# First-layer jobs of twice the tiles in an attention and gated feed-forward kernel: one PSUM unit of gates and one of values

## The chip, the cores and the metric

The kernel runs on one core of a Trainium2 chip. The metric is the device time of one execution in microseconds (us); less is better. The names of the profile: PE is TensorE (matmuls) and PEld its weight loads, DVE is VectorE, ACT is ScalarE, POOL is GpSimd, SP is SyncE.

## The reference

Two computations follow each other. First an attention with a block mask, over 4 batches, 8 heads, 768 positions and 64 columns a head; then a feed-forward network with a sigmoid gate over the 3072 tokens.

```python
scores = np.matmul(q, k.transpose(0, 1, 3, 2)) / np.sqrt(64)
scores = np.where(mask, scores, -1e9)    # blocks of 32: neighbours, first and last, 3 sampled ones a row
attn = softmax(scores)                   # over the keys
x = np.matmul(attn, v)                   # -> (3072, 512), heads side by side
gate = 1.0 / (1.0 + np.exp(-(x @ w_gate)))       # 512 -> 1536
out = (gate * (x @ w_val)) @ w_out               # 1536 -> 512
```

## The kernel before

**Units.** The 3072 tokens are 12 units of 256: unit n is a third of the queries of batch n // 3. For each unit and each pair of heads (0 to 3) there are three tasks of scores, `s4.3.2` being unit 4, pair 3, third 2 of the keys. Each is four matmuls into a PSUM unit, one exp of 1024 columns on ACT (L597) that empties it into a buffer P, and, when the three thirds are there, one product of 3072 columns with the mask on DVE (L624). Then come the product of P and v (`pv`), the division by the sums of rows (`nrm`, L649 and L650) and the transposition of x.

**First layer.** `f2.1` is job 1 of group 2. Units 1 to 4 are groups of their own; 5 and 6, 7 and 8, 9 and 10 are groups 5 to 7; `GROUPS` has the list. Before the change a job is one PSUM unit of two banks: one bank takes the gate's products (x times w_gate), the other the values' (x times w_val), 512 columns each, which is two tiles of 128 hidden columns for one unit, or one for a pair. TensorE has 16 matmuls for each half a job. ACT makes a tanh of 512 columns from the gates (L823; the sigmoid is half of 1 plus the tanh of half the input), and DVE multiplies it with the values into `ht` (L826, "the gate" below), after which the PSUM unit is free.

**Second layer.** Units 1 to 10 go in pairs, with seven products in place of eight (`z1` is units 1 and 2, `z2` units 3 and 4, `z4` units 7 and 8; in it A, B, P5, P4 and P3 are products, c11 to c22 what goes out). The sums of blocks that they need are made on DVE (L962, tiles `sums` and `wsum`). Unit 0 (`y0`) and unit 11 (`y_last`) go alone.

**Row tiles.** Most matmuls contract over 64 rows, and two of them stand side by side in the two row halves of the array (`64*128` in the profile). They are recorded by `turns`, in halves a and b, since the two row halves change PSUM banks between them; other work is put in between. The first layers of units 0 and 1 (`WIDE = 2`) use all 128 rows (`128*128`), recorded by `whole`.

**PSUM** is four units of two banks, `m0` to `m3` (m_125 to m_128 where instructions are listed). Whoever takes one waits until its last reader is done.

**The order** is written by hand. All pieces are tasks in a list of class `Plan`; the string `ORDER` says in which order they are recorded. In a token such as `41:3` or `234@249` the number is the task, a letter behind it the engine on which it is done, `:3` the PSUM unit that it takes, and `@249` holds a load until task 249's scores. Each engine runs its own instructions in that order:

```python
            if slot is not None:
                more["take"].slot = int(slot)
            self.last[i] = fn(eng or engines[0][0])
            if gate is not None:
                self.hold(self.last[i], self.last[int(gate)])
```

**Loads and copies.** q, k and v and the weights come by DMA from POOL's queue (L220, L230, L235). POOL, ACT or DVE copy k and q (to `pr`, L277 and L279) and v (to `vex`); k is then transposed by a DMA (`kT<-pr`). For the last unit half of w_out, which the sums of the pairs have overwritten, is loaded again (L1086).

Of the kernel before, what the change touches and what calls it, by code (L numbers as in the profile page):

```python
# [23 lines left out]
NP = H // 2  # L24
# [12 lines left out]
SPLIT, AFTER = 3, (0, 1, 3, 2)  # L37
BIG = 1024.0
# [4 lines left out]
j3 j3 j3 j3 j3 j3 j3 j3 6 17 14 11A 7:0 18:3 8 15:2 19A 16 9:1 23:0 38:3 39 40:2 24 10 21:0 41 86:1  # L43
26:3 87A 82:2 22 27 42:0 46:1 43 47 83 12:3 31:2 13 32 33:0 34 36:3 37 84:2 28:0 62:1 63 85 50:2 51
29 70:0 96@70 20 88:3 44:1 30 71 89 52:2 72:3 90:0 45 73 56:1 91 53 74:3 4@56 0@56 3@56 25 149@56 75
60:2 66:0 80:3 81 57 61 54:1 92:2 48:3 67 111:0 93 112 55 113:1 114 225@113 49 64:3 35 97:2 76:0 65
125@113 98 106:3 77 107 68:1 78:2 69 121:0 79 99:1 122 58:3 100 59 144:2 145 165:1 123:3 124 115
130:0 131 126:2 132 133 147:3 146 166 148 103:0 127 138:1 128 104 134:3 2@103 139 129 109:1 110
1@103 94:0 163:2 135 95 136 179:1 180 164 137 153:0 105 182:1 5@182 154 251:2 252 150:3 183 193:2
151 194 155 167 240:0 241 156:1 152 157 117:2 201 108@240 184:3 191 185 118 187:0 192 158 249:2 202  # L50
169:1 223:3 188 250 140:0 170 224 141 205:2 189:0 171 198@205 206 161G 190 243:3 244 199:0 200 195
172 159:2 258 160A 221:0 173 162 203:3 101:2 186@203 102 245@203 142G 143 238G 222 174 204 218:0 177
196:2 175D 197 259 253 276:3 219 277 207 212:1 282:2 213 214 260A 242 247G 283 209:3 210 211 215:1
261 265:2 216 235 217 266 239 168@265 236 237 273:3 255:1 263:2 274 264 256 119:0 268 120 284:3 269
270 248 285 116@284 328:0 275 329 279 246 229:2 230 231 286 363:1 220G 361:3 362 364 232:0 208@361
325:2 233 326 305:3 226:1 181 234 254@305 300:0 287@305 303:2 306 365 278@303 257G 330@303 227 228
262G 301 304 320 446@303 389:3 449G 390 321 327 322 292:1 380:2 381 293 294 295 331 367:3 410:2 358
178 368 375 432:0 411 280G 370:1 433 376 377 371 296:2 372:0 373 297 267@372 332 366@372 298 333 386
299 383:3 384 288:1 391:0 392 289 316:2 290 302G 435:3 317 382 312:0 437@435 291 412:1 385@412 436
318 681@412 307@412 393 319 323G 313 176 413 314 315 407:3 441:1 442 408 460:2 427 308:0 461 434  # L60
443:1 428 309 444 463:2 399:1 429 438 450:3 310 311 464 335 336 447:0 530:2 281 451 400 445 448
338:3 531 401 402 337 414@530 457:2 324 339 374@457 454 458 341 532:1 533 342 347:2 271G 359A 369
455 272 343 589@532 387G 456 452:1 340 482:0 334 344 348 346 349 453 353:1 459 483 345 539:0 504:3
350 540 430G 505 354 465:0 466 351 484:3 355 378G 395:1 501:0 485 352 480:2 388 467 396 537:3
597@537 481 502 561@537 498 360 397 538 462 398 564G 419:0 503 547:1 548 499 500 558:3 559 420 421
472:1 379 575:2 439 576 422 565:3 473 535:0 566 403:2 536 529 567:3 440 474 534 431 475 404 550:1
542 568 490:3 405 406 394@550 409G 617@550 551 543 544 593:2 491 549 594 492 493 556:1 415:0 553
578:2 557 560 416 579 417 418 423:1 586:3 587 562:2 424 563 425 584:3 585 476:0 426 570 614:1 615
603:3 577 604 571 572 477 468:1 588 581 606:2 478 479 590:3 607 469 591 470 471 598 595:2 596
552@595 599 600 658:0 486:1 605 612:2 696G 554G 633:3 487 632G 659 660@633 613 634 494:0 630:2 495  # L70
488 496 616 489 655:3 497 631 650 506 357 656 592 609 618:1 651 652 676:0 677 507 619 620 356 638:3
580@676 678:0 541@678 639 733:2 679 621 509:1 608@733 640 641 734 747:0 748 742:3 508 510 512D 518:2
582G 583 743 513 511 635:0 727:3 636 569@727 519 514 728 735:0 736 697:3 698 515 516 657 517 626:0
520 740:3 627 730:1 741 628 521 680 694:3 731 629 545G 546 601G 522 695 699:1 674A 700 673 523 755:0
724 555 524:2 725 756 737 767:1 602 768 525 726 622:0 526 753:3 573 574 754 729 661:1 623 624 610
625 646:2 662 663 738:3 750:0 751 647 739 664 648 770:1 744 669:0 649 760:2 771 637@760 527 761 745
762:1 763 670 749 746 671 672 642:2 682:1 643 644 773:3 774 758:0 683 757 759 645 764 848:3 684
665:2 765 752 685 849 686:1 675 666 667 766 769 775:0 668 687 690:3 776 611 688 790:0 653G 654 831:2
691 791 832 777 808 689 811:2 692 693 701 702 772 732 812 778:1 829:3 830 809 850:2 779 851 780 810
782:3 893:2 894 781 704:0 814:1 792:2 793 528 705 703 707D 708 783 815 784 794:2 800:1 795 709 878:2  # L80
# [5 lines left out]
962:0 963 856 864:2 854 926:1 858D 859 921:0 927 922 865 860 920 943:1 945:0 903 944 857 946 861 863  # L86
# [4 lines left out]
1029 1038 1049 1005 1006:0 1031:2 1007 1032 1033 1050 1030 1015:3 1009D 1010 1039:1 1011 1040 1041  # L91
1012 1034 1016 1042 1014 1021:2 1043:1 1008 1017 1022 1018 1023 1025 1044 1026 1019 1045 1013D 1020
1051:2 1052 1046 1053 1054 1056:0 1057 1058 1061:3 1062 1063 1024 1059 1055 1064 1065 1060
# [58 lines left out]
def kernel(  # L152
# [214 lines left out]
    def whole(mms, bank, begins=True, ends=True):  # L367
# [21 lines left out]
    rings["xT"] = [xTs[:, (n + 1) % 6] for n in range(6)]  # L389
    used = {nm: {} for nm in rings}  # L390
# [388 lines left out]
    class Ffn:  # L779
# [16 lines left out]
        def f(self, j):  # L796

            bank = Bank()
            i = len(used["th"])
            th = home("th", i)  # L800
# [77 lines left out]
            c = plan.add(f"f{self.g}.{j}.th", [(ACT, 0.57)], tanh, [a] + before("th", i), free=bank, part=1)  # L878
            g = plan.add(f"f{self.g}.{j}.ga", [(DVE, 0.68)], gate, [c], free=bank, part=1)
            used["th"][i] = [g]  # L880
            for f in tiles:
                self.gated[f] = g
# [65 lines left out]
        def z(self, mate):  # L948
# [132 lines left out]
            if self.z_ == last_z:  # L1081
                back.append(
                    plan.add(
                        "ldw0",
                        [(DMA, 0.72)],
                        lambda eng: nc.gpsimd.dma_start(  # L1086
                            wo[:, 0:HF, UQ : 2 * UQ],
                            moe_w_out.rearrange("(f p) m -> p f m", p=128)[:, 0:HF, UQ : 2 * UQ],
                        ),
                        [pb, t3],  # L1090
                        dma=("L", 0.393),
                    )
                )
# [22 lines left out]
        def y_last(self, i):  # L1116

            n = self.ns[i]
            for s, c0, c1, eng, queue in (
# [6 lines left out]
                for f0 in range(0, NF, 4):  # L1126

                    def go(eng, bank=bank, f0=f0, s=s, c0=c0, c1=c1):
                        for f in range(f0, f0 + 4):
                            tiled(  # L1130
                                both(bank)[:, 0, 0 : c1 - c0],
                                self.ht[:, f, i * UQ + s * 128 : i * UQ + (s + 1) * 128],
                                wo[:, f, c0:c1],
                                f == 0,
                                f == NF - 1,
                            )

                    a = plan.add(
                        f"y{n}.{s}.{c0}.{f0}",
                        [(PE, 4 * Y_WIDE * (c1 - c0) / DM)],  # L1140
                        go,
                        [self.gated[f] for f in range(f0, f0 + 4)] + (back if a is None else [a]),
                        take=bank if f0 == 0 else None,
                        lag=0.0 if f0 < 8 else None,
                        ops=8,
                        wide=True,
                    )
# [188 lines left out]
```

## Time and profile before

| | |
|---|---|
| runs | 282.92, 284.26 and 290.8 us; median 284.26 |
| the profiled execution | 282.64 us, of which 280.9 us is the span of the core |
| clock granted to TensorE in the span | 0.994 |
| instructions | 11919, of them 5459 matmuls, 282 on DVE, 231 on ACT |

The profile is one execution. In its rows a matmul's end is modelled; the starts are measured. "Idle before" is the time in which an engine stood still ahead of an instruction, with the name of what ended it; a line of waits has the total, the number and the longest. Stages: to 27.46 us masks, first loads and scores; from there the first layer of unit 0; at 45.09 its second layer begins; to about 160 us attention and both layers mixed; after that the last pairs' layers.

### The profile page before, as it was taken

How to read it: one execution, taken by the hardware profiler on the slowest of the kernel's cores; microseconds unless marked ns; L12 is line 12 of the kernel's file. 1: busy time of each engine (PE TensorE's matmuls, PEld its weight loads, DVE VectorE, ACT ScalarE, POOL GpSimd, SP SyncE). 2: the span in 40 equal slices, each digit the busy share in tenths (PEclk: the TensorE clock that was granted, in tenths of full speed). 3: DMA queues.
4: the chain of work that ended last, by engine and by line, in shares of the span. 5: the costliest groups of instructions: out<-in, count | busy, mean ns of one | idle time of the engine just before them, and what ended most of it. 6: DMA issues, size and time to landing. Idle time of an engine off the chain costs nothing.

```text
span 280.9 us, 11919 instructions
## 1 busy us (share of the span) xinstructions
PE 270.7 (96%) x5459; PEld 208.6 (74%) x5459; DVE 210.6 (75%) x282; ACT 187.7 (67%) x231; POOL 76.9 (27%) x98
## 2 busy tenths in 40 slices
PE   6899999999899989999999999999999999999995
PEld 2677886777789869889787666678656876759983
DVE  4568685879998998689978877977669868537371
ACT  2699888789799768889788676875765753323100
POOL 8966432345756552222451012000000000000010
PEclk9799999999999999999999999999999999999999
DMA  7999999969879897854899338200330401040063
GB/s 152 181 195 196 200 203 156 130 106 144 119 138 131 124 182 66 105 74 109 140 120 122 94 56 119 97 2 5 126 44 5 57 5 77 2 116 0 2 133 149
DMA packets 55434, 29.36 MB, mean 105 GB/s; under 512 B 32308, under 2 KB 53708, under 8 KB 55384
## 3 DMA queue, kind: packets, MB, share of 16 engines
q0 software_dynamic: 22384, 14.33, 37.6%
q1 hardware_dynamic: 32512, 13.98, 27.5%
q8 instruction: 42, 0.69, 1.0%
q10 hardware_dynamic: 488, 0.30, 0.3%
q14 instruction: 8, 0.07, 0.1%
HBM read 29.25 MB, written 6.29 MB: 127 GB/s over the span
## 4 chain that ended last, share of the span: by engine, by line
PE 71%; DMA 14%; POOL 6%; DVE 4%; ACT 2%; issue 1%; ACTq 0%; POOLq 0%
PE m L337 71%; DMA wv<-in_moe_w_val_dram 7%; DMA wo<-in_moe_w_out_dram 3%; DMA q<-in_q_dram 2%; DMA kT<-pr 2%; DVE P L624 2%; POOL k L220 1%; POOL q L220 1%; ACT P L597 1%; DVE ht L826 1%; POOL v L220 1%; POOL wg L230 1%; DVE sums L962 1%; ACT th L823 1%; POOL wv L230 1%
## 5 line engine op out<-in xcount | busy, mean ns | idle before, releaser
L597 ACT ACTIVATE P<-m 128x1024 f16<-128x1024 f32 x144 | 142.2, 1024 | 31.9 <-PE m L337 30.2
L337 PE MATMUL m<-xTs,wg 64*128 64x256 f16 (+2 forms) x768 | 137.8, 310 | 0.3 <-DVE ysb L1103 0.2
L337 PE MATMUL m<-xTs,wv 64*128 64x256 f16 (+2 forms) x768 | 137.9, 310 | 0.0
L337 PEld LDWEIGHTS <-wg 64*128 64x128 f16 (+1 forms) x768 | 70.4, 94 | 16.1 <-issue 1.7
L624 DVE TENSOR_TENSOR P<-P,mask 128x3072 f16<-128x3072 f16 x44 | 80.9, 1845 | 1.2 <-ACT P L597 1.2
L337 PEld LDWEIGHTS <-wv 64*128 64x128 f16 (+1 forms) x768 | 70.2, 94 | 14.9 <-issue 0.4
L823 ACT ACTIVATE th<-m 128x512 f32<-128x512 f32 x72 | 42.8, 599 | 45.0 <-PE m L337 44.6
L826 DVE SCALAR_TENSOR_TENSOR ht<-th,m 128x512 f16<-128x512 f32 x72 | 48.7, 683 | 30.5 <-ACT th L823 30.1
L337 PE MATMUL m<-qT,kT 64*128 64x256 f16 x576 | 53.8, 271 | 1.4 <-DMA kT<-pr 0.9
L337 PEld LDWEIGHTS <-P 64*128 64x128 f16 (+1 forms) x2112 | 44.9, 94 | 8.2 <-issue 1.7
L337 PE MATMUL m<-vex,P 64*128 64x65 f16 (+1 forms) x2112 | 48.3, 190 | 1.2 <-DVE P L624 0.8
L337 PE MATMUL m<-wo,ht 64*128 64x256 f16 (+3 forms) x444 | 41.6, 284 | 0.1
L337 PEld LDWEIGHTS <-ht 64*128 64x128 f16 (+1 forms) x564 | 35.3, 94 | 6.2 <-DVE wsum L962 0.5
L337 PEld LDWEIGHTS <-kT 64*128 64x128 f16 x576 | 26.5, 94 | 11.0 <-issue 2.6
L1086 POOL DMA_DIRECT2D wo<-in_moe_w_out_dram x1 | 0.8, 840 | 97.2 <-PE m L337 97.2
L337 PEld LDWEIGHTS <-sums 64*128 64x128 f16 x360 | 23.3, 94 | 2.9 <-issue 0.4
L1027 DVE SCALAR_TENSOR_TENSOR ysb<-m,ysb 128x512 f32<-128x512 f32 x25 | 17.2, 689 | 7.3 <-PE m L337 4.9
L220 POOL DMA_DIRECT2D q<-in_q_dram x19 | 13.9, 729 | 19.6 <-PE m L337 12.3
L650 DVE TENSOR_TENSOR x16s<-m,rz 128x512 f16<-128x512 f32 (+1 forms) x28 | 17.2, 615 | 1.0
L220 POOL DMA_DIRECT2D k<-in_k_dram x15 | 10.9, 724 | 23.2 <-PE m L337 22.0
L279 POOL COPY pr<-k 128x768 f16<-128x768 f16 x9 | 10.6, 1188 | 19.6 <-DMA kT<-pr 11.7
L337 PE MATMUL m<-early,sums 64*128 64x256 f16 x120 | 14.7, 269 | 0.1
(63 smaller groups left out, 167.3 us busy)
## 6 DMA issues: line engine op xcount, KB each, us to landing
out_dram<-ysb SPq DMA_DIRECT2D x10, 512.0 KB, 2.9
v<-in_v_dram POOLq DMA_DIRECT2D x16, 192.0 KB, 4.9
k<-in_k_dram POOLq DMA_DIRECT2D x15, 192.0 KB, 5.0
q<-in_q_dram POOLq DMA_DIRECT2D x12, 192.0 KB, 4.9
wg<-in_moe_w_gate_dram POOLq DMA_DIRECT2D x6, 256.0 KB, 8.2
wv<-in_moe_w_val_dram POOLq DMA_DIRECT2D x6, 256.0 KB, 9.1
wo<-in_moe_w_out_dram POOLq DMA_DIRECT2D x6, 256.0 KB, 9.7
out_dram<-ysb SPq DMA_DIRECT2D x3, 256.0 KB, 3.3
```

What stands on the lines that cost most here:

```text
L220: return nc.gpsimd.dma_start(dst[:, h0:h1, t0:t1, :], src[b, h0:h1].rearrange("h (p t) d -> p h t d", t=NT)[:, :, t0:t1, :],)
L230: nc.gpsimd.dma_start(dst[:, :, f0:f1], src.rearrange("(c p) f -> p c f", p=128)[:, :, f0:f1])
L279: nc.gpsimd.tensor_copy(dst, src)
L337: return nc.tensor.matmul(out, lhsT, rhs, start=start, stop=stop, skip_group_check=True).ins
L597: nc.scalar.activation(self.pt.rearrange("a h i n -> a h (i n)"), both(self.bank), AF.Exp, bias=0.0, scale=SCALE)
L624: nc.vector.tensor_tensor(pt, pt, m.unsqueeze(1).broadcast_to([128, 2, NT * UQ]), op=ALU.mult)
L650: nc.vector.tensor_tensor(self.x16, acc[:, :, :, 0:D], rz.broadcast_to([128, w, 2, D]), op=ALU.mult)
L823: nc.scalar.activation(th, both(bank)[:, 0, :], AF.Tanh, bias=0.0, scale=0.5)
L826: nc.vector.scalar_tensor_tensor(self.ht[:, tiles[0] : tiles[-1] + 1, :], in0=th.rearrange("a (f n) -> a f n", n=self.w), scalar=1.0, in1= ...
L962: nc.vector.tensor_tensor(dst, x, y_, op=op)
L1027: nc.vector.scalar_tensor_tensor(dst, in0=src(), scalar=0.5, in1=add, op0=ALU.mult, op1=ALU.add)
L1086: lambda eng: nc.gpsimd.dma_start(wo[:, 0:HF, UQ : 2 * UQ], moe_w_out.rearrange("(f p) m -> p f m", p=128)[:, 0:HF, UQ : 2 * UQ],),
```

## The change

Groups 1 to 7 use a job of another form, `twin`. One PSUM unit holds 1024 columns of gates, another 1024 columns of values. Each has its two halves (xa and xb for the gates, ya and yb for the values). One tanh of 1024 columns empties the gates' unit and frees it; one product of 1024 columns empties the values' unit. 60 jobs become 30. The three buffers of tanh become one tile `ths` of three parts, of which a twin always uses the first two, so that a twin's tanh waits for the gate of the twin before. Unit 1's first layer is in row tiles like those of units 2 to 10. The second copy of half of w_out (`reload`) goes to the place of the keys, `k16`, which is free when the last pair is copied, and not to its old one; `y_last` cuts six matmuls of 512 columns in two for it. `ORDER` is new all over.

```diff
+TWIN = range(1, 8)
 ORDER = """
-j3 j3 j3 j3 j3 j3 j3 j3 6 17 14 11A 7:0 18:3 8 15:2 19A 16 9:1 23:0 38:3 39 40:2 24 10 21:0 41 86:1
+j3 j3 j3 j3 j3 j3 j3 j3 6 7:0 11 14A 15:1 9:2 17A 8 18:3 16A 19 10A 12:0 21:1 23:3 125 13A 24 40:2
...
-            ("th", 3, [128, 2 * UQ], f32),
+    ths = sing.tile([128, 3, 2 * UQ], f32, name="ths")
+    gating = [[], [], []]
...
+        def twin(self, j):
+
+            gates, vals = Bank(), Bank()
+            th = ths[:, 0:2].rearrange("a i n -> a (i n)")
+            f0 = 2 * self.per * j
...
+            def tanh(eng):
+                nc.scalar.activation(
+                    th, both(gates).rearrange("a g n -> a (g n)"), AF.Tanh, bias=0.0, scale=0.5
+                )
+
+            def gate(eng):
+                nc.vector.scalar_tensor_tensor(
+                    self.ht[:, f0 : f0 + 2 * self.per, :],
+                    in0=th.rearrange("a (f n) -> a f n", n=self.w),
+                    scalar=1.0,
+                    in1=both(vals).rearrange("a g (f n) -> a (g f) n", n=self.w),
+                    op0=ALU.add,
+                    op1=ALU.mult,
+                )
...
+            x = product("x", gates, wg, self.xs)
+            c = plan.add(key + "th", [(ACT, 1.02)], tanh, [x] + gating[0] + gating[1], free=gates)
+            v = product("y", vals, wv, self.xs)
+            g = plan.add(key + "ga", [(DVE, 1.22)], gate, [c, v] + before("ht", self.z_), free=vals)
+            self.read += [x, v]
+            gating[0] = gating[1] = [g]
...
-            if self.z_ == last_z:
-                back.append(
-                    plan.add(
-                        "ldw0",
...
+                            parts = [(c0, c1)] if f >= HF or c1 - c0 == UQ else [(0, UQ), (UQ, DM)]
+                            for a, b in parts:
...
+                                    wo12[:, f, :] if f < HF and a == UQ else wo[:, f, a:b],
...
+    wo12 = k16.rearrange("a h t d -> a (h t d)")[:, 0 : HF * UQ].rearrange("a (f m) -> a f m", m=UQ)
+
+    def reload():
...
+                [x for p in range(NP) for x in copies["k", B - 1, p]],
...
+        if g in TWIN:
+            for j in range(NF // per // 2):
+                parts.append((g, [start] * (j == 0) + [lambda ns=ns, j=j: made[ns[0]].twin(j)]))
```

What the new order does is seen best in the instructions themselves. First TensorE, at the first job of unit 1. Before:

```order
L337 MATMUL m_125<-vex_81,P_132 128x65
L337 LDWEIGHTS wg
L337 MATMUL m_126<-xTs,wg 128x256
L337 LDWEIGHTS wv
L337 MATMUL m_126<-xTs,wv 128x256
```

and now:

```order
L336 MATMUL m_126<-vex_81,P_132 128x65
L336 LDWEIGHTS wg
L336 MATMUL m_128<-xTs,wg 128x256
L336 LDWEIGHTS wg
L336 MATMUL m_128<-xTs,wg 128x256
```

Gates and values took turns in one PSUM unit (m_126); now the gates alone fill m_128, and the values come later in a unit of their own.

Second POOL's queue between the last weights of the first layer and the first copies of batch 1, with the loads of w_out (`wo`, six of them). Before:

```order
L220 DMA k_76<-in_k_dram 128x2x384
L235 DMA wo<-in_moe_w_out_dram 128x2x512 x3
L220 DMA q_75<-in_q_dram 128x2x384
L220 DMA k_76<-in_k_dram 128x2x384 x2
L235 DMA wo<-in_moe_w_out_dram 128x2x512 x3
L220 DMA q_75<-in_q_dram 128x2x384 x2
```

and now:

```order
L219 DMA k_76<-in_k_dram 128x2x384
L234 DMA wo<-in_moe_w_out_dram 128x2x512
L219 DMA q_75<-in_q_dram 128x2x384
L219 DMA k_76<-in_k_dram 128x2x384
L234 DMA wo<-in_moe_w_out_dram 128x2x512 x5
L278 COPY pr_139<-k_76 128x768
L278 COPY pr_136<-q_75 128x768
```

Ahead of the last load of w_out stood four loads of q and k; now there are three, of which two more stand ahead of the second load of w_out. The two loads of q behind have moved down, and copies of k and q follow at once.

Third ACT at unit 2's first layer. Before (L597 are exps of scores, L823 tanhs):

```order
L597 ACTIVATE P_131<-m_128 128x2x512
L597 ACTIVATE P_131<-m_125 128x2x512
L823 ACTIVATE th_134<-m_126 128x512
L597 ACTIVATE P_133<-m_128 128x2x512
L823 ACTIVATE th_136<-m_127 128x512
L597 ACTIVATE P_132<-m_126 128x2x512
L823 ACTIVATE th_135<-m_125 128x512
```

and now (L598 and L909), from the tanh of f2.1 to that of f2.2 and the exp of s4.3.2 behind it:

```order
L909 ACTIVATE ths<-m_125 128x1024
L598 ACTIVATE P_132<-m_127 128x2x512
L598 ACTIVATE P_129<-m_126 128x2x512
L598 ACTIVATE P_133<-m_127 128x2x512
L276 COPY pr_138<-q_75 128x768
L598 ACTIVATE P_131<-m_127 128x2x512
L598 ACTIVATE P_130<-m_125 128x2x512
L909 ACTIVATE ths<-m_128 128x1024
L598 ACTIVATE P_133<-m_126 128x2x512
```

Three tanhs of 512 columns, each with a buffer of its own, stood between four exps; now two of 1024 share one buffer, with five exps and a copy of q between them.

More of the change, by code (lines that the diff above doesn't have):

```diff
@@ L48 @@
[L48 to L64, printed above, removed]
@@ new lines @@
+398:0 531 363G 409 525 526 549:1 551@549 550 399 400 575:3 404:1 419 576 532:0 534@532 405 403 428
+560:3 406 533 459:2 544:0 561 568:1 569 545 542 594:3 460 552 559 585:1 553 535 595 586 456:3 554
+566:1 457 563 567 458 543@566 462:0 461 577:1 578 463 464 339 437G 465:3 621:1 572:2 466 523@621
+596:0 570 467 622 536G 597 573 580 681:1 581 623:3 682 468:0 582 624 588:1 589 471:2 537 469 690:3
+470 587 618:1 472 619 691 598 644 697:0 698 652:3 653 579@652 473 480 645 481 555 591 600:2 649:0
+650 646 601 483:3 625@649 602 683:0 482 527G 528 712:1 713 484 609:2 492:1 654@712 486D 487 684
@@ L94 @@
+958 987 990 991 997:3 988 992 998 999 1000 1007:2 1008 1009 1001 1002:0 1003 1004 1005 1006 1010
+1011
 """
@@ L798, in f @@
             bank = Bank()
-            i = len(used["th"])
-            th = home("th", i)
+            i = nth[0] % 3
+            nth[0] += 1
+            th = ths[:, i]
             tiles = range(self.per * j, self.per * (j + 1))
@@ L877, in f, with half, go, product @@
             self.read.append(a)
-            c = plan.add(f"f{self.g}.{j}.th", [(ACT, 0.57)], tanh, [a] + before("th", i), free=bank, part=1)
+            c = plan.add(f"f{self.g}.{j}.th", [(ACT, 0.57)], tanh, [a] + gating[i], free=bank, part=1)
             g = plan.add(f"f{self.g}.{j}.ga", [(DVE, 0.68)], gate, [c], free=bank, part=1)
-            used["th"][i] = [g]
+            gating[i] = [g]
             for f in tiles:
+                self.gated[f] = g
+        def twin(self, j):
+            gates, vals = Bank(), Bank()
+            th = ths[:, 0:2].rearrange("a i n -> a (i n)")
+            f0 = 2 * self.per * j
+            def half(bank, w, first):
+                def go(eng):
+                    mms = []
+                    for o in range(self.per):
+                        for c in range(4):
+                            mms.append(
+                                lambda g, rows, o=o, c=c: (
+                                    both(bank)[:, g, o * self.w : (o + 1) * self.w],
+                                    w[rows, c, (f0 + g * self.per + o) * 128 : (f0 + g * self.per + o + 1) * 128],
+                                    self.x[rows, :, c, :],
+                                )
+                            )
+                    turns(mms, bank, first)
+                return go
+            def tanh(eng):
+                nc.scalar.activation(
+                    th, both(gates).rearrange("a g n -> a (g n)"), AF.Tanh, bias=0.0, scale=0.5
+                )
+            def gate(eng):
[6 more added lines that the diff above has]
+                    op1=ALU.mult,
+                )
+            key = f"f{self.g}.{j}."
+            def product(name, bank, w, deps):
+                a = plan.add(
+                    key + name + "a", [(PE, F_HALF)], half(bank, w, True), deps, take=bank, lag=GAP, ops=16 * self.per
+                )
+                return plan.add(key + name + "b", [(PE, F_HALF)], half(bank, w, False), [a], ops=16 * self.per)
+            x = product("x", gates, wg, self.xs)
[4 more added lines that the diff above has]
+            gating[0] = gating[1] = [g]
+            for f in range(f0, f0 + 2 * self.per):
@@ L1129, in go @@
                         for f in range(f0, f0 + 4):
[L1130 to L1136, printed above, removed]
+                            parts = [(c0, c1)] if f >= HF or c1 - c0 == UQ else [(0, UQ), (UQ, DM)]
+                            for a, b in parts:
+                                tiled(
+                                    both(bank)[:, 0, a - c0 : b - c0],
+                                    self.ht[:, f, i * UQ + s * 128 : i * UQ + (s + 1) * 128],
+                                    wo12[:, f, :] if f < HF and a == UQ else wo[:, f, a:b],
+                                    f == 0 and a == c0,
+                                    f == NF - 1,
+                                )
                     a = plan.add(
@@ L1215, in later @@
                 loads.append(lambda nm=nm, p=p: load(nm, p))
+    wo12 = k16.rearrange("a h t d -> a (h t d)")[:, 0 : HF * UQ].rearrange("a (f m) -> a f m", m=UQ)
+    def reload():
+        back.append(
+            plan.add(
+                "ldw0",
+                [(DMA, 0.72)],
+                lambda eng: nc.gpsimd.dma_start(
+                    wo12, moe_w_out.rearrange("(f p) m -> p f m", p=128)[:, 0:HF, UQ : 2 * UQ]
+                ),
+                [x for p in range(NP) for x in copies["k", B - 1, p]],
+                dma=("L", 0.393),
+            )
+        )
     def do(queue, fn):
@@ L1253 @@
         per = 512 // (UQ * len(ns))
-        for j in range(NF // per):
-            parts.append((g, [start] * (j == 0) + [lambda ns=ns, j=j: made[ns[0]].f(j)]))
+        if g in TWIN:
+            for j in range(NF // per // 2):
+                parts.append((g, [start] * (j == 0) + [lambda ns=ns, j=j: made[ns[0]].twin(j)]))
+        else:
+            for j in range(NF // per):
+                parts.append((g, [start] * (j == 0) + [lambda ns=ns, j=j: made[ns[0]].f(j)]))
         z, i = place[ns[-1]]
@@ L1302 @@
     do(turned, Pair.xt)
+    reload()
     while parts:
```

68 lines of the change are left out of this document (34 added, 34 removed), and 17 rows, old and new, of the table ORDER.

## The prediction

> **What bounds the kernel now.** I read the engine shares first, then the busy time by stage, then TensorE's waits, and last the rows around each wait.
>
> ```profile
> span 280.9 us, 11919 instructions
> PE 270.7 (96%) x5459; PEld 208.6 (74%) x5459; DVE 210.6 (75%) x282; ACT 187.7 (67%) x231; POOL 76.9 (27%) x98
> ...
> core 0: us, PE busy (x) PEld busy (x) DVE busy (x) ACT busy (x) POOL busy (x), PEclk, DMA share, GB/s
> 0.00:27.46 27.46, 23.86 (x465) 15.49 (x466) 16.95 (x47) 19.18 (x22) 21.43 (x34) 0.94 1.24 181
> 27.46:45.09 17.63, 17.54 (x238) 13.94 (x238) 13.52 (x21) 15.10 (x19) 6.25 (x9) 1.00 1.35 202
> 45.09:110.00 64.91, 62.15 (x1426) 51.38 (x1427) 56.09 (x63) 53.92 (x65) 32.61 (x37) 1.00 0.96 127
> 110.00:160.00 50.00, 49.64 (x1194) 41.71 (x1190) 43.22 (x51) 41.16 (x50) 13.37 (x17) 1.00 0.70 103
> 160.00:277.80 117.80, 117.52 (x2146) 86.11 (x2142) 80.85 (x103) 57.99 (x77) 3.26 (x3) 1.00 0.26 61
> ```
>
> TensorE is busy 117.52 of 117.80 us in the last stage and 49.64 of 50.00 in the one before. Only the stretch 45 to 110, in which batches 1 and 2 are loaded and their attention is mixed with the first layers of units 1 to 4, leaves 2.76 us. ACT and DVE have 11 and 9 us of slack there. A saving on them pays only where one of them ends a wait of TensorE.
>
> Whether "busy" means full has to be seen in single rows, since ends of matmuls are modelled:
>
> ```profile
> 71.96 0.27 PE L337 MATMUL m<-xTs,wg 64*128 64x256 f16 x1
> 71.96 0.27 PE L337 MATMUL m<-xTs,wv 64*128 64x256 f16 x1
> ...
> 72.83 0.38 PE L337 MATMUL m<-qT,kT 64*128 64x256 f16 x4
> ```
>
> One half of a job is 16 such matmuls. They start at 71.96 and the next work starts at 72.83: 0.87 us, 54 ns each, though each is drawn as 0.27. So the starts are the measure, and a wait that the profile shows as n costs up to 0.16 more (0.27 drawn, less 0.11 between two pairs).
>
> [...] The waits are thus the whole of what I count as open.
>
> ```profile
> PE m L337 <- DMA kT<-pr: 0.9, 1, 0.9
> PE m L337 <- DVE P L624: 0.8, 1, 0.8
> PE m L337 <- DVE ht L826: 0.4, 2, 0.2
> PE m L337 <- DVE ysb L1027: 0.3, 1, 0.3
> PE m L337 <- DVE ysb L1103: 0.2, 1, 0.2
> PE m L337 <- DVE wsum L962: 0.2, 1, 0.2
> ```
>
> From 27 us to the end these are all: 2.8 us in 7 waits, with 7 x 0.16 about **3.9 us**.
>
> **The change, part by part.**
>
> *Fewer, longer instructions: 0 by themselves.*
>
> ```profile
> L597 ACT ACTIVATE P<-m 128x1024 f16<-128x1024 f32 x144 | 142.2, 1024 | 31.9 <-PE m L337 30.2 <-DVE rz L649 0.5
> L823 ACT ACTIVATE th<-m 128x512 f32<-128x512 f32 x72 | 42.8, 599 | 45.0 <-PE m L337 44.6
> L826 DVE SCALAR_TENSOR_TENSOR ht<-th,m 128x512 f16<-128x512 f32 x72 | 48.7, 683 | 30.5 <-ACT th L823 30.1
> L650 DVE TENSOR_TENSOR x16s<-m,rz 128x512 f16<-128x512 f32 x20 | 13.8, 691 | 0.7
> L650 DVE TENSOR_TENSOR x16s<-m,rz 128x256 f16<-128x256 f32 x8 | 3.4, 424 | 0.3
> ```
>
> 60 tanhs of 0.60 become 30, each about as long as an exp of 1024 columns, 1.02: ACT saves 5.3 us. For the product, 256 columns more cost 0.267 on DVE (691 - 424), so 512 more cost 0.53: 1.22 us (estimate), and DVE saves 30 x (2 x 0.683 - 1.22) = 4.4 us. TensorE hides both. What matters is that a gate now takes 1.22 instead of 0.68 before anyone can use it.
>
> *Unit 1 in row tiles: -1.0.* Its matmuls of 128 rows become twice as many of 64.
>
> ```profile
> 54.38 0.27 PE L337 MATMUL m<-xTs,wg 128*128 128x256 f16 x1
> 54.49 0.27 PE L337 MATMUL m<-xTs,wv 128*128 128x256 f16 x1
> 54.70 0.39 PE L337 MATMUL m<-qT,kT 64*128 64x256 f16 x4
> 55.02 0.28 PE L337 MATMUL m<-xTs,wg 128*128 128x256 f16 x1
> ```
>
> A 128-row matmul starts every 0.11, as a pair of 64-row ones does: the work is equal. But from 128 rows to 64 it takes 0.21 (54.49 to 54.70), and back 0.32 where four scores of 54 ns need 0.22: 0.10 at each switch. Six jobs with scores between make about ten switches: -1.0, bounds 0 and -1.2.
>
> *The waits: -3.9.* The seven stand at other work now, since the whole order is new. The largest:
>
> ```profile
> 68.99 1.75 DVE L624 TENSOR_TENSOR P<-P,mask 128x3072 f16<-128x3072 f16 x1
> 71.86 2.98 DVE L624 TENSOR_TENSOR P<-P,mask 128x3072 f16<-128x3072 f16 x1 [0.43 <-ACT P L597]
> 73.27 2.25 POOL L279 COPY vex<-v 128x768 f16<-128x768 f16 x1
> 74.90 0.54 PE L337 MATMUL m<-vex,P 64*128 64x65 f16 x24 [0.79 <-DVE P L624]
> 102.98 0.61 PE L337 MATMUL m<-qT,kT 64*128 64x256 f16 x8 [0.88 <-DMA kT<-pr]
> 57.22 0.83 ACT L277 COPY pr<-q 128x768 f16<-128x768 f16 x1 [1.82 <-DMA q<-in_q_dram]
> ```
>
> A mask product beside a POOL copy takes 2.98 instead of 1.75, and TensorE waits for it; the new POOL order puts other work there. The k of batch 2 came 0.88 late; by the new order about 1.1 us more matmuls lie between its copy and its use. The q copy that held ACT for 1.82 us goes to POOL. I take all seven as gone and charge what is late next below.
>
> *The start: -0.4.* More of the first copies are on ACT, and the order of first scores is new. But the second layer of unit 0 cannot start before w_out:
>
> ```profile
> 35.59 9.46 DMA wo<-in_moe_w_out_dram
> ...
> 45.09 0.83 PE m L337 x8
> ```
>
> The DMA share until there is 1.24 and 1.35, so the loads set this point, and in the new order of POOL's loads only the places of single q and k loads among them change. Bounds: -0.83, the first part of y0 (x8, 0.83 us), which alone can be drawn ahead before the later parts of w_out bind; and +0.97, one more q load (192 KB at 202 GB/s) ahead of w_out. I take -0.4, half of the first, since more of TensorE's 3.6 idle us before 27.46 are open than that.
>
> *The reload of w_out for the last unit: 0.*
>
> ```profile
> L1086 POOL DMA_DIRECT2D wo<-in_moe_w_out_dram x1 | 0.8, 840 | 97.2 <-PE m L337 97.2
> ```
>
> POOL stood idle for 97.2 us ahead of it and nothing was queued behind; it now leaves as soon as the last k pair is copied, into that pair's buffer. The 6 matmuls that y_last has more are 6 of 512 columns cut in two: the same columns, so 0. If this cover fails (the load late), y_last would wait, but it has over 100 us for a transfer that took 9.46 in a full queue.
>
> *What the twins add: +3.5.* A gate's unit comes back after the modelled end of the last matmul (0.27 - 0.11), the product and a hand-over:
>
> ```profile
> 59.49 1.30 DVE ht L826 x2
> 60.79 0.04 issue
> 60.83 6.69 PE m L337 x150
> ...
> L962 DVE TENSOR_TENSOR sums<-ht 128x1536 f16<-128x1536 f16 x5 | 5.0, 1009 | 0.2
> L962 DVE TENSOR_TENSOR sums<-sums,ht 128x1536 f16<-128x1536 f16 x5 | 4.8, 955 | 0.1
> ```
>
> That is 0.16 + 1.22 + two hand-overs of 0.04 and a queue place, about 1.6 us. The distances are counted in the new order at 54 ns a matmul:
>
> - Units 2 and 3: scores s4.3.2 and s6.1.0 take the unit of f2.1's and f3.1's values 20 matmuls (1.07 us) after these: 0.55 each, **+1.1** (0 to 2.1).
> - One tanh buffer: f2.2's tanh stands in ACT's queue behind f2.1's product, and the exp of s4.3.2 behind it; f3 alike. The delay above covers most: **+0.2** (0 to 1.6).
> - Beside second layer z1 only one unit is left for scores. A score gives it back after 1.02 + 0.16 + 0.06 = 1.24; s5.0.1 comes 0.72 after s5.3.2, and the neighbours 1.28: **+0.6** (0 to 1.25).
> - z1, z2 and z4 start 3.07, 3.44 and 3.38 us of matmuls after the last values. The chain is 1.6 + 1.01 + 0.96 = 3.57, and up to 3.85 with DVE's queue: 0.5 + 0.3 + 0.2 = **+1.0** (0 to 2.5). z2's evictions come in the same way: **+0.3**.
> - Three loads of batch 1, not two, are held until s2.3.1: **+0.3** (0 to 1.5, the late k above with its 0.88 as a middle).
>
> Sum: -1.0 - 3.9 - 0.4 + 3.5 = -1.8. The profiled execution took 282.64 us (span 280.9 and 1.74 around it); the median of the three runs is 284.26, 1.6 higher, so that the profiled one lies at their low end. 282.64 - 1.8 = 280.8; since the new kernel is timed by a median too, I say **281.0 us**, 1.1% under the median of before. A difference under 2% can hardly be told from none by this measurement.
>
> **The rivals.**
>
> *All waits are gone and none comes* (R1). 282.64 - 5.3 = **277.3**, with the bounds of start and switches (0.83 and 1.2) 276.7. For it: after 110 us TensorE has only 0.6 us that are not busy, so orders without waits exist for three fifths of the work, and the longer instructions leave ACT and DVE more slack to hide a late one. Against it: five distances above are shorter than the durations that they must cover, and only an earlier start of ACT or DVE than I read from the rows could mend that. 0.24.
>
> *TensorE starves for PSUM units* (R2, the other side). From f1 to z4 one job holds two of the four units at once, and a second layer holds two more for its sums; then a score, a job's values and a normalisation all wait for the one unit that comes back. The price is that of the upper bounds, 2.1 + 1.6 + 1.25 + 2.5 + 0.3 + 1.5 = 9.3 instead of 3.5, with the gains as above: 282.64 - 5.3 + 9.3 = **286.6**. It decides from the point at which a returned gate has less than 1.6 us of other matmuls ahead of its next user, at more than the two places counted. For it: 1.07 at two places, and 1.43 at the last jobs of units 2 and 3. Against it: the other gates of units 1 to 3 have 1.7 to 3.6 in the new order, a tanh gives its unit back before the product begins, and ACT and DVE have 5.3 and 4.4 us less to do. 0.11.
>
> [...]
>
> *Collisions of POOL copies with mask products come elsewhere* (R3). Each costs 1.23 (2.98 - 1.75); one or two without cover give 282.0 to 283.3. It ends within 2%, and so does the case that TensorE's saturation leaves nothing to win at all (282.6). 0.20 together.
>
> **How the numbers follow.** Forecast (279 to 282) 0.45, R1 0.24, R3 and nothing 0.20, R2 0.11. 2% under the median is 278.6, 2% above it 289.9. R1 alone falls under the first: faster **0.24**. R2 passes the second only where the old waits also stay (286.6 + 3.9 = 290.5); I give that 0.07, so slower **0.07** and no difference **0.69**. The range reaches from R1 with part of its bounds to R2's price: **276.5 to 286.6**; what is left out is R2 beyond its price and a little of R1, some 0.12.
>
> **What the new profile would show.** TensorE busy 96% or more, about 5561 matmuls. Waits for the gate at units 2 and 3 of about half a microsecond, and one at each of z1 and z2 on the sums. A tanh near 1.02 and a product near 1.22 confirm the prices; a product of 0.9 or less would free the units before their users come and take the +1.1 and +1.0 back. No gap of 0.21 at unit 1's jobs, no wait for k near 103. The waits that TensorE has between 45 and 110 should add to about as much as before, on other releasers (the gate L914, the sums L1018, the exp L598). I am wrong to the fast side if there are none, and to the slow side if waits on exps or gates are found after 110 us, where I count nothing beyond z4's 0.2.

## The result and the profile after

The changed kernel takes 286.51 us in the median (286.27 to 287.14); against the kernel before the ratio is **1.0131** (95% interval 1.0099 to 1.0163). It is slower by 1.3%, where 281.0 us was forecast. The interval compares like runs of both kernels only: three of the six executions of the kernel before ran some 3% longer, none of the changed kernel did, and those three are left out. The profiled executions are 286.52 us after and 282.64 us before: 3.9 us to explain.

First the page, then the busy time by stage (columns as before), then the longest of TensorE's waits from 27 us on:

```profile
span 284.8 us, 12066 instructions
PE 272.1 (96%) x5561; PEld 213.6 (75%) x5561; DVE 206.1 (72%) x254; ACT 184.7 (65%) x199; POOL 79.5 (28%) x98
...
45.00:110.00 65.00, 63.14 (x1567) 53.99 (x1565) 55.99 (x63) 53.89 (x57) 26.36 (x31) 1.00 0.96 135
110.00:160.00 50.00, 49.91 (x1170) 42.45 (x1166) 41.41 (x45) 38.91 (x41) 17.60 (x18) 1.00 0.65 98
160.00:190.42 30.42, 30.28 (x647) 19.16 (x645) 23.57 (x23) 22.15 (x23) 3.09 (x4) 1.00 0.62 87
190.42:199.26 8.84, 6.28 (x105) 5.61 (x103) 6.54 (x8) 3.07 (x3) 0.00 (x0) 0.81 0.13 34
199.26:281.70 82.44, 82.09 (x1402) 63.12 (x1398) 50.40 (x57) 32.01 (x36) 0.00 (x0) 1.00 0.15 50
...
PE m L336 <- DVE ysb L1083: 2.9, 2, 2.6
```

TensorE is as full as before in every stage but one: the 8.84 us from 190.42, where it is busy for 6.28 and its clock falls to 0.81. There stands a wait of 2.6 us for DVE's L1083, at a place where the kernel before had no wait. What led to it, engine by engine (POOL, SP, DVE, TensorE):

```profile
180.43 0.71 POOL L219 DMA_DIRECT2D v<-in_v_dram  x1 [4.60 <-PE m L336]
181.14 0.85 POOL L1269 DMA_DIRECT2D k<-in_moe_w_out_dram  x1
...
182.40 1.21 SPq L712 DMA_TRANSPOSE xTs<-x16s  x1
183.66 0.59 SPq L1131 DMA_DIRECT2D out_dram<-ysb  x1
...
183.66 8.14 DMA out_dram<-ysb
...
191.90 0.69 DVE L1146 TENSOR_SCALAR ysb<-m 128x512 f32<-128x512 f32 x1 [3.96 <-DMA out_dram<-ysb]
192.62 0.69 DVE L1083 SCALAR_TENSOR_TENSOR ysb<-m,ysb 128x512 f32<-128x512 f32 x1
...
190.42 0.39 PE L336 MATMUL m<-qT,kT 64*128 64x256 f16 x4
193.37 1.59 PE L336 MATMUL m<-wo,ht 64*128 64x256 f16 x24 [2.56 <-DVE ysb L1083]
196.24 2.37 PE L336 MATMUL m<-wo,ht 64*128 64x256 f16 x24
198.43 0.83 PE L336 MATMUL m<-wsum,sums 64*128 64x256 f16 x12
```

Read from the end: z3's product B needs the sums that DVE makes at L1146 and L1083 out of product A. DVE stood still for 3.96 us, since L1146 writes the place from which z2's second store was still being sent. That store left at 183.66 and took 8.14 us. Beside it ran a load of v (180.43) and, from 181.14, the reload of w_out (L1269), which the change moved here from 267.6 us.

The stall has a second part. The 24 matmuls from 196.24 take 2.19 us, where such a group takes 1.31. The granted clock (the column behind POOL's), in short stretches behind the wait:

```profile
194.00:195.00 1.00, 1.00 (x20) 0.94 (x18) 1.00 (x2) 0.00 (x0) 0.00 (x0) 0.81 0.00 0
195.00:196.00 1.00, 1.00 (x30) 0.96 (x28) 1.00 (x1) 0.58 (x1) 0.00 (x0) 0.50 0.00 0
196.00:197.00 1.00, 1.00 (x14) 0.85 (x10) 0.96 (x4) 0.94 (x2) 0.00 (x0) 0.50 0.00 0
197.00:198.43 1.43, 1.43 (x21) 1.27 (x19) 0.88 (x2) 0.53 (x1) 0.00 (x0) 0.64 0.08 17
```

The clock is at half for about 3.4 us in all (an estimate from these four rows: 0.4, 1, 1 and 1.0 us) and full again from 199.26 us on (first view). So the place costs 2.73 us of stall (the four scores from 190.42 need 0.22) and about 1.6 us of slow work, 4.4 in all: more than the whole difference.

### The profile page after: what moved, and what is told of

Same layout as the page of the kernel before. It is cut to its first block, busy times and chain, and to the rows that moved or that the text cites. A ratio compares the mean times of both kernels' runs of the same rounds, so it can differ in the third digit from the quotient of the medians.

```text
span 284.8 us, 12066 instructions
## 1 busy us (share of the span) xinstructions
PE 272.1 (96%) x5561; PEld 213.6 (75%) x5561; DVE 206.1 (72%) x254; ACT 184.7 (65%) x199; POOL 79.5 (28%) x98
## 4 chain that ended last, share of the span: by engine, by line
PE 76%; DMA 11%; POOL 4%; DVE 4%; ACT 2%; issue 2%; DVEq 0%; SPq 0%; ACTq 0%; POOLq 0%
PE m L336 75%; DMA q<-in_q_dram 3%; DMA out_dram<-ysb 3%; DMA wg<-in_moe_w_gate_dram 3%; DMA qT<-pr 2%; ACT P L598 1%; POOL pr L278 1%; DVE ht L914 1%; DVE ysb L1083 1%; POOL v L219 1%; POOL q L219 1%; POOL k L219 1%; DMA k<-in_k_dram 1%; DVE sums L1018 1%; DVE ysb L1146 0%
## 5 line engine op out<-in xcount | busy, mean ns | idle before, releaser
L598 ACT ACTIVATE P<-m 128x1024 f16<-128x1024 f32 x144 | 142.4, 1024 | 50.0 <-PE m L336 48.1
L336 PE MATMUL m<-xTs,wv 64*128 64x256 f16 (+2 forms) x816 | 84.4, 307 | 0.0
L336 PE MATMUL m<-xTs,wg 64*128 64x256 f16 (+2 forms) x816 | 84.2, 307 | 0.1
L336 PEld LDWEIGHTS <-wg 64*128 64x128 f16 (+1 forms) x816 | 47.3, 94 | 15.2 <-issue 0.8
L336 PEld LDWEIGHTS <-wv 64*128 64x128 f16 (+1 forms) x816 | 47.9, 94 | 13.2
L914 DVE SCALAR_TENSOR_TENSOR ht<-ths,m 128x1024 f16<-128x1024 f32 x30 | 36.5, 1218 | 17.8 <-PE m L336 12.0
L336 PE MATMUL m<-wo,ht 64*128 64x256 f16 (+2 forms) x438 | 42.0, 289 | 2.6 <-DVE ysb L1083 2.6
L909 ACT ACTIVATE ths<-m 128x1024 f32<-128x1024 f32 x30 | 30.7, 1024 | 19.4 <-PE m L336 10.8
L1083 DVE SCALAR_TENSOR_TENSOR ysb<-m,ysb 128x512 f32<-128x512 f32 x25 | 17.3, 690 | 13.2 <-PE m L336 10.9
L219 POOL DMA_DIRECT2D v<-in_v_dram x16 | 11.6, 732 | 43.2 <-PE m L336 37.5
L825 ACT ACTIVATE ths<-m 128x512 f32<-128x512 f32 x12 | 7.1, 597 | 18.1 <-PE m L336 17.6
L278 POOL COPY pr<-q 128x768 f16<-128x768 f16 x9 | 13.4, 1486 | 5.3 <-DMA qT<-pr 2.9
```

What stands on the lines that cost most here:

```text
L219: return nc.gpsimd.dma_start(dst[:, h0:h1, t0:t1, :], src[b, h0:h1].rearrange("h (p t) d -> p h t d", t=NT)[:, :, t0:t1, :],)
L278: nc.gpsimd.tensor_copy(dst, src)
L336: return nc.tensor.matmul(out, lhsT, rhs, start=start, stop=stop, skip_group_check=True).ins
L598: nc.scalar.activation(self.pt.rearrange("a h i n -> a h (i n)"), both(self.bank), AF.Exp, bias=0.0, scale=SCALE)
L825: nc.scalar.activation(th, both(bank)[:, 0, :], AF.Tanh, bias=0.0, scale=0.5)
L909: nc.scalar.activation(th, both(gates).rearrange("a g n -> a (g n)"), AF.Tanh, bias=0.0, scale=0.5)
```

## The experiments

**Is it the reload?** One task is moved in the order, the load of w_out.

```diff
-... 795 972 839:2 ...        ... 871:0 872 ...
+... 795 839:2 ...            ... 871:0 972@871 872 ...
```

> The changed kernel with one token moved: the reload of w_out is held until scores s11.0.1 (near 214 us) and no longer leaves at 181 us. Theory A (the reload shares the transfer engines with the store of layer z2's second unit, which then takes 8.1 us instead of about 3, and TensorE waits for the place that this store empties, after which its clock is low for some 4 us): the store lands in 3 to 4 us, the wait of 2.6 us and the half clock behind it go, and the execution takes 286.5 - 4.2 = 282.3 us. Theory B (the store is late because it stands behind a transposition in SP's queue; the reload is a bystander): the store still leaves at 183.7; if that alone made it late, a wait of 1 us or more stays and the time is 285 or more. Theory C (the twins starve TensorE of PSUM units, and the wait near 193 only shows it): another wait of 2 us or more comes near the same place, 286 us.

Median 283.5 us (281.32 to 285.52), ratio 1.0009 (0.9959 to 1.0058); profiled execution 282.07. The store still leaves at the same time (SP), and DVE now waits only for TensorE:

```profile
183.71 0.57 SPq L1131 DMA_DIRECT2D out_dram<-ysb  x1
...
188.17 0.69 DVE L1146 TENSOR_SCALAR ysb<-m 128x512 f32<-128x512 f32 x1 [0.19 <-PE m L336]
...
190.36 1.48 PE L336 MATMUL m<-wo,ht 64*128 64x256 f16 x24
193.78 0.82 PE L336 MATMUL m<-wsum,sums 64*128 64x256 f16 x12
...
DMA to landing us min/median/max: 2.6/3.3/4.0
```

The last line is that of the stores (L1131) from 150 us on: none takes more than 4.0 us now, where one took 8.1. The work from B to `wsum` takes 3.42 us in place of 5.06. Theory A's time came in the profiled execution, within 0.3 us; the median is 1.2 above it. B alone and C are out: the store left no earlier (183.71), and no other wait came in its place.

**Or the place of the store in SP's queue?** The store waited in that queue behind a transposition of unit 9, which itself waits for DVE. Now the store is ahead of it, and the reload is where the change had it:

```diff
-... 501 831:0 826 ... 758 502 661D ...
+... 501 502 831:0 826 ... 758 661D ...
```

> The changed kernel with one token moved: SP issues the store of z2's second unit before the transposition of unit 9 and not behind it; the reload stays at 181 us. Theory A with B as a condition (both are needed: a late store and a reload beside it): the store leaves some 9 us earlier and lands before the reload starts, the wait near 193 us goes, 282.3 us. Theory A alone (whenever the reload runs, something else that it shares the engines with comes late): 284 us or more, with a wait on another transfer. Theory C: 286 us.

Median 282.32 us (281.35 to 283.44), ratio 0.9963 (0.9937 to 0.9988). Both stores leave together, from 173.69 us on (the second left at 183.66), and B starts as soon as the scores ahead of it are done (190.66 and 0.22):

```profile
173.69 0.81 SPq L1131 DMA_DIRECT2D out_dram<-ysb  x2
...
190.66 0.39 PE L336 MATMUL m<-qT,kT 64*128 64x256 f16 x4
190.88 1.48 PE L336 MATMUL m<-wo,ht 64*128 64x256 f16 x24
```

So it takes two things together, a store that leaves late and a load beside it; taking away either is enough. The reload still slows what runs beside it: the transposition of unit 9, sent between 182.4 and 182.8 us, takes 8.3 us in the changed kernel, 7.6 here and 4.0 in reload_late, but TensorE does not wait for it. Why transfers take twice as long side by side, no run here shows. This version is faster than both kernels, than the one before by only 0.4% (0.1% to 0.6%).

**The reload alone, in the kernel before.** `y_last` and the load as in the change, the load's task directly behind the last copy of keys; all else as before.

```diff
-                            wo[:, 0:HF, UQ : 2 * UQ],
+                            wo12, ...
-                        [pb, t3],
+                        [x for p in range(NP) for x in copies["k", B - 1, p]],
...
-... 653G 654 ...     ... 1026 ...
+... 653G 1026 654 ...
```

> The kernel before with the reload alone: into the place of the keys, issued as soon as the last keys are copied (near 170 us), with y_last's six matmuls cut in two; all else in its old order. Theory A with B as a condition (the old order sends z2's second store before its product p1 needs the place, at 185 us, some 4 us early): the store may take longer but nothing waits for it; same as before within 0.5 us, 282.6, or 0.2 better for the wait at the very end (272 us) that goes. Theory A alone (an early reload always makes a store late): 285 us or more.

Median 284.4 us of the runs compared (283.25 to 286.72), ratio 1.0032 (0.9979 to 1.0085): not told apart from before. But the trace has a victim after all, another one than I looked for, in the waits and in the chain that ended last:

```profile
PE m L337 <- DMA kT<-pr: 2.1, 2, 1.4
...
170.82 7.17 DMA kT<-pr
```

The new one of these two waits is 1.4 us near 178 us: the transposition of the last keys, sent right beside the reload (170.39), took 7.17 us, where it took 3.6 in the kernel before. The stores passed without harm, as A with B said; "nothing waits" was wrong. So a late store is not the only thing that the load can hurt: it cost TensorE time in both places where a transfer beside it had no slack.

**Does the clock fall because TensorE stood still?** The wait is left, but twelve matmuls without use are put into it.

```diff
-... 829:1 663 830 851:3 ...
+... 829:1 830 w1 w1 w1 w1 w1 w1 663 851:3 ...
```

> The changed kernel with the wait near 193 us left in, but 12 matmuls without use (512 columns, into a PSUM unit that is free then, some 1.3 us) put ahead of it. Theory of the clock (TensorE's clock is lowered for some 4 us because it stood still for 2.6 us): the wait ends at the same time, 193.3 us, but the work behind it runs at full clock, so that some 1.4 us are won: 285.1 us. Rival (the half clock belongs to the work or the time, not to the idle stretch): 286.5 us or a little more, with the granted clock at 0.5 from 195 to 197 as now.

Median 285.86 us (285.21 to 287.2), ratio 1.0087 (1.0049 to 1.0125); profiled execution 285.21, 1.3 less than the changed kernel's.

```profile
191.25 1.47 PE L314 MATMUL m<-wg 64*128 64x512 f16 x12 [1.11 <-ACT P L599]
193.04 1.49 PE L337 MATMUL m<-wo,ht 64*128 64x256 f16 x24 [0.32 <-DVE ysb L1084]
...
196.46 0.83 PE L337 MATMUL m<-wsum,sums 64*128 64x256 f16 x12
...
195.00:196.00 1.00, 1.00 (x27) 1.00 (x21) 0.97 (x3) 1.00 (x2) 0.00 (x0) 1.00 0.00 0
```

B still starts near 193, but the clock stays at 1.00, and the work behind takes 3.42 us as in reload_late: 1.64 less. The half clock does come from the idle stretch. The other executions agree: over the span all six of the changed kernel have a granted clock of 0.982 to 0.994 (3.4 us at half lower this mean by 0.006), here eight of ten have 1.000. The two others, the profiled one among them, have 0.994; in that one the half clock lies near 10 us (last section). In time the gain is less clear: the ratio falls from 1.0131 to 1.0087, about 1.2 us, and the two intervals overlap.

**The price of a switch.** Unit 1's twins with 128 rows again, on reload_late:

```diff
-                    turns(mms, bank, first)
+                    if self.ns == (1,):
+                        mms = [m for i, m in enumerate(mms) if (i % 4 < 2) == first]
+                        whole(mms, bank, first, not first)
+                    else:
+                        turns(mms, bank, first)
```

> The changed kernel with the reload held late, and unit 1's three twins with matmuls of 128 rows as in the kernel before (half the number, each half of a job taking half of the sum); all else as in reload_late. Theory of the prediction (each change between 128 and 64 rows costs TensorE 0.10 us): twelve halves with other work between them make about 20 switches, +1.5 to +2.2 us in the stretch of unit 1 and 284 us where reload_late had 282 in its profiled execution. Rival (a switch is hidden, or the old gaps there came from other waits): no difference, within 0.3 us in that stretch.

Median 286.09 us (285.5 to 286.56), ratio 1.012 (1.006 to 1.018). One half of a job and its neighbours, in reload_late and then here:

```profile
51.88 1.05 PE L336 MATMUL m<-xTs,wg 64*128 64x256 f16 x16
52.75 0.40 PE L336 MATMUL m<-qT,kT 64*128 64x256 f16 x4
...
52.24 1.05 PE L336 MATMUL m<-xTs,wg 128*128 128x256 f16 x8
53.22 0.39 PE L336 MATMUL m<-qT,kT 64*128 64x256 f16 x4
```

The half takes 0.87 us in the one and 0.98 in the other, up to the scores. The starts of all matmuls of unit 1's stretch have 22 such gaps of 0.10 us here, 2.2 us, against 7 in the kernel before (and three longer ones). From the first of these jobs to that of unit 2 it is 21.46 us in reload_late and 23.26 here, +1.8, with about as much of waits in the one (0.97) as in the other (0.93). The price stands. The medians differ by 2.6 us (on two chips). The profiled execution takes 285.93 us, where 284 was expected; it has two more waits of 0.67 us (100.12, on DVE) and 1.12 us (220.10, without a releaser), which I can't assign.

**One tanh buffer or two**, on reload_late:

```diff
-    ths = sing.tile([128, 3, 2 * UQ], f32, name="ths")
+    ths = sing.tile([128, 4, 2 * UQ], f16, name="ths")
...
-            th = ths[:, 0:2].rearrange("a i n -> a (i n)")
+            h = 2 * (ntw[0] % 2)
+            ntw[0] += 1
+            th = ths[:, h : h + 2].rearrange("a i n -> a (i n)")
```

> The changed kernel with the reload held late, and with two places of 1024 columns for the tanh, used in turn, so that a twin's tanh no longer waits for the gate of the twin before (in f16, since two in f32 do not fit); all else as in reload_late. ACT's 8.4 us of waits of the tanh on the gate should go. Theory of the prediction (+0.2 for the one buffer, since the delay of the values' unit covers it): 0 to -0.3 us. Rival (the one buffer holds up the exps behind it on ACT, and these TensorE): -0.8 us or more, with the waits on exps near 97 and 102 us gone. If the product reads f16 faster than f32, that shows as a mean under 1.22 us and has to be taken off.

Median 282.44 us of the runs compared (281.78 to 284.13), ratio 0.9984 (0.9949 to 1.0019); profiled execution 282.44 against 282.07. ACT's waits, of reload_late and then here:

```profile
ACT ths L909 <- DVE ht L914: 8.4, 5, 4.2
...
ACT ths L912 <- PE m L336: 17.7, 13, 4.3
```

8.4 us of waiting for the gate change their name and no gain is seen: ACT then waits for TensorE instead, and TensorE's wait of 0.2 us on an exp near 97 us is still there. The product takes 1.219 us in the mean, 1.218 in the changed kernel, so reading f16 changes nothing in it.

**What comes next, once the reload does no harm?** Three runs on the start and the keys of batch 1. In late_q_turn the work from `74` on is put in another order:

```diff
-62:3 72:1 45 63 74:0 70:2 71 73 92:1 75 108@92 80:0 96@92 81 54:3 93 66:0 67 111:2
+62:3 72:1 45 63 70:2 71 80:0 73 92:1 81 108@92 96@92 54:3 74:2 75 93 66:0 67 111:2
```

> The changed kernel with the reload held late (as in reload_late), and a change of the first 25 us alone: the transposition by TensorE of the second part of q's heads 2 and 3 (qt1.2), which stood waiting for its load from 18.3 to 19.7 us, is put behind a mask product, scores of unit 0 and a product with v, some 1.6 us of matmuls later; all else as in reload_late. Theory (that early place is why the start of the changed kernel is 0.8 us longer): the wait of 1.3 to 1.5 us near 19 is gone or under 0.3, the first layer of unit 0 starts 0.7 to 1.4 us earlier than in reload_late, and the execution is 0.5 to 1 us shorter. Rival (the loads of q and of the first layer's weights set the pace, whatever stands first): another load is waited for instead, near 26 us, and the first layer starts within 0.3 us of where it did.

> The changed kernel, reload at 181 us as it is, with three moves in the order: z2's second store ahead of the transposition of unit 9 (as in store_first), the late transposition of q at the start (as in late_q_turn), and the store of unit 0's first half directly behind that of its second half (near 81 us instead of 92 us). Theory: the wait near 193 us stays away, the first layer of unit 0 starts near 27.0 us, the wait for this store beside z1 (0.2 to 0.9 us near 97 us) goes; but what the start wins is given back at the keys of batch 1 (kT<-pr, 1.4 us near 62 us, as in late_q_turn), so that the profiled execution is 281.5 to 282.5 us, same as before within 1%. Rival (the start's gain is kept): 281 us or less, with less than 0.7 us of waits for keys near 62 us.

> As three_moves, and the three loads of batch 1 that were held until scores s2.3.1 (near 50 us) are held until s2.1.0 only (near 46 us). Theory (these keys' way, load, copy and transposition by DMA, sets the pace near 62 us once the start is faster): the wait there falls from 1.4 us to 0.3 or less, and the execution is 1 us shorter than three_moves: 280.5 to 281.5 us. Rival (transfers are shared: w_out and the other keys come later in return): the wait moves to another transfer between 45 and 70 us, and the time is that of three_moves within 0.4 us.

Medians 282.53, 282.16 and 282.07 us; ratios 0.9967 (0.9924 to 1.001), 0.9964 (0.9924 to 1.0004) and 0.9972 (0.9943 to 1.0002). First the start of unit 0's first layer and the wait for keys in reload_late, then in late_q_turn and in three_moves:

```profile
27.65 0.27 PE L336 MATMUL m<-xTs,wg 128*128 128x256 f16 x1
61.44 0.61 PE L336 MATMUL m<-qT,kT 64*128 64x256 f16 x8 [0.46 <-DMA kT<-pr]
...
27.01 0.27 PE L336 MATMUL m<-xTs,wg 128*128 128x256 f16 x1
61.64 0.61 PE L336 MATMUL m<-qT,kT 64*128 64x256 f16 x8 [1.31 <-DMA kT<-pr]
...
27.62 0.27 PE L336 MATMUL m<-xTs,wg 128*128 128x256 f16 x1
61.86 0.61 PE L336 MATMUL m<-qT,kT 64*128 64x256 f16 x8 [0.92 <-DMA kT<-pr]
```

In late_q_turn the start is 0.64 us earlier, but the keys, which come at 61.4 to 61.9 whatever the start is, are waited for 0.85 us longer. The 0.5 to 1 us of the theory are not won: the profiled execution takes 283.07 us, 1.0 more than that of reload_late. In three_moves the start is at 27.62 again, since the next q load is waited for 1.14 us at 25.81: the rival of late_q_turn. In loads_early the keys are no longer waited for, but the start is still later (27.97), and the profiled execution takes 282.85 us, against 282.61 of three_moves: the rival there. In these profiles it is the loads that set the pace of the first 60 us, and none of the three runs won more than store_first alone.

## Why the prediction was wrong, step by step

- **"The reload of w_out for the last unit: 0"** is the step that failed. I asked who waits for this load (y_last, 96 us later: right) and not what else is on the transfer engines at its new time. It costs 2.73 us of stall and 1.6 us of half clock, 4.4 in all. Without that, in store_first, the time is 282.32 us, 1.3 above the forecast: 0.4% under the kernel before, where I had forecast 1.1%.
- *The start: -0.4.* Not found, and read from the wrong load. Unit 0's first layer begins at 28.23 in the changed kernel's profile and at 27.46 in that of before, its second layer at 45.43 and 44.40. So 45.09 was not the beginning: there w_out held one pair of the second layer's matmuls by 0.25 us. The load that leads to the start is one of q (first row: before; behind it: the chain that ended last in the changed kernel):

```profile
44.40 1.30 PE L337 MATMUL m<-wo,ht 64*128 64x512 f16 x8
...
17.93 8.44 DMA q<-in_q_dram
...
28.23 17.23 PE m L336 x234
```

  In all nine profiles with the new order the first layer starts some 1.85 us after such a load has landed, and the second layer 17.20 us after the first, without a wait for w_out. The starts of the other eight, some with the start altered, lie between 27.01 and 27.97, and before_reload, with the old order, is at 28.56: they scatter by more than the term.
- *Unit 1 in row tiles: -1.0.* Right in kind and price. Of the ten switches three stand in longer gaps (0.36 to 0.43 us between two starts), which hold something else too; the other seven cost 0.10 us each: -0.7, within the bounds.
- *The waits: -3.9.* All seven are gone from their places; near 103 us TensorE waits for no k.
- *What the twins add: +3.5.* The prices of tanh and product were right:

```profile
L914 DVE SCALAR_TENSOR_TENSOR ht<-ths,m 128x1024 f16<-128x1024 f32 x30 | 36.5, 1218 | 17.8 <-PE m L336 12.0
L909 ACT ACTIVATE ths<-m 128x1024 f32<-128x1024 f32 x30 | 30.7, 1024 | 19.4 <-PE m L336 10.8
...
85.41 1.04 PE L336 MATMUL m<-xTs,wv 64*128 64x256 f16 x16
...
87.83 0.40 PE L336 MATMUL m<-qT,kT 64*128 64x256 f16 x4
```

  1.22 and 1.02 us, as estimated. At unit 2 the last values start at 85.41 and end after 0.87; the scores s4.3.2 follow at 87.83, 1.55 later with 1.07 of work between: 0.48, where I had 0.55. At unit 3 it is 0.50. (The list of waits shows neither, since the modelled ends of the matmuls cover them.) The one tanh buffer, +0.2, is not seen (two_tanh). The loads of batch 1, +0.3, cost 1.0 here and 0.4 to 1.4 in the other runs, within their bounds. What z1, z2 and z4 add one by one, no run shows.

  All terms but the reload and the start come to 3.9 - 4.4 - 0.8 = -1.3 us by difference, where I had -1.4. That they come so close is in part luck: from the start of unit 0's first layer to the end, reload_late is 0.8 us shorter than the kernel before and store_first 0.2.
- **The rivals.** R1 is refuted (new waits did come), and so is R2 as a mechanism, though its 286.6, the upper end of my range, is by chance the time: the stall is on a store, not on a PSUM unit, and goes with the reload while the twins stay. Of R3's collisions little came: the longest mask product is 2.38 us (2.98 before), and no wait of TensorE is on one.

## What to carry to other kernels

When a transfer is moved, look at what else is in flight at its new time and which of these has a waiter with little slack; cover for its own reader says nothing of that. A store that stands in its queue behind an instruction that waits is late before it starts (183.66 us here, 173.69 ahead of that instruction), so send first what frees a buffer. A wait of an engine that is otherwise full can cost more than its length (1.6 us more for 2.56 here): read the granted clock behind it.

## What the runs showed that I had not expected

An idle stretch of 2.56 us on TensorE was followed, 1.2 us after work began again, by 3.4 us at half clock, worth 1.6 us. In before_reload a stretch of 1.44 us, which ends at 178.04, was not. But in filled one of 1.26 us near the start was followed by half clock too:

```profile
178.04:179.00 0.96, 0.96 (x12) 0.58 (x14) 0.19 (x1) 0.53 (x1) 0.00 (x0) 1.00 1.23 395
...
7.90 0.38 PE L480 MATMUL m<-const,k 64*64 64x64 f16 x24 [1.26 <-DMA k<-in_k_dram]
...
9.00:12.00 3.00, 3.00 (x58) 1.97 (x56) 1.79 (x4) 2.08 (x3) 2.77 (x4) 0.50 1.38 191
...
7.66 0.26 PE L478 MATMUL m<-const,q 64*64 64x64 f16 x8 [0.69 <-DMA q<-in_q_dram]
...
9.00:11.00 2.00, 1.85 (x56) 1.31 (x56) 1.22 (x4) 1.92 (x3) 2.00 (x4) 0.50 1.33 186
```

The first row is of before_reload (clock 1.00), the next two are of filled (clock 0.50), the last two of the kernel before (clock 0.50). It has such a stretch of half clock there too, near 10 us, behind a wait of 0.69 us; it is why its clock is 0.94 in the first stage. So the length of one idle stretch does not decide alone. What else goes into it, no run here shows.
